# Reading an expert's first weights in 4 KB runs instead of 8 KB runs

## The chip, the core and the metric

The kernel runs on one core of a Trainium2 chip. The metric is the time of one execution on the device, in microseconds, as the median of several runs. A core has a matrix engine (TensorE, PE in the profile; its weight loads are listed as PEld), a vector engine (VectorE, DVE), a scalar engine (ScalarE, ACT), a general engine (GpSimd, POOL) and SyncE (SP), each with its own instruction queue. They share an on-chip memory of 128 partitions (SBUF) and an accumulation memory that TensorE writes to (PSUM). Data comes from the chip's large memory, and goes back to it, by DMAs that run on 16 DMA engines.

## What is computed

Attention over 8 batches with 8 heads, 576 positions and a head dimension of 64, in FP32. Half of the heads use a plain causal window of 32, the other half a causal window of 128 with a dilation of 4. Its output, put together as 4608 rows of 512, goes into a soft mixture of 8 experts with 4 slots each:

```python
logits = x @ phi
d = softmax of logits over the rows
slot_input = d.T @ x                       # 32 slots x 512
for e in range(8):
    h = np.maximum(slot_input[e] @ w1[e], 0.0)   # 512 -> 1024
    slot_out[e] = h @ w2[e]                      # 1024 -> 512
c = softmax of logits over the slots
out = c @ slot_out                         # 4608 x 512
```

The expert weights are w1 with 8 x 512 x 1024 values and w2 with 8 x 1024 x 512, all in FP32 in memory.

## The kernel before

Every load is a DMA issued from POOL's queue. It reads FP32 and writes FP16, so 4 KB in SBUF is 8 KB in the large memory. The output is converted the other way. There are about a hundred DMAs, and they use eight completion semaphores in turn: a DMA that takes a semaphore waits until the DMA that had it before, eight issues earlier, has landed. So no more than about eight loads are under way, and POOL waits at most of its issues.

The order of the program is written out by hand (a schedule with `slot0`, `slot1` and `slot2` for every batch, L565 to L649). While batch b is computed, the loads for batch b + 2 are issued: q and k (`load_qk`, L133) in `slot0`, v (`load_v`, L147 and L150) in `slot1`. Between them `weights` (L531) issues one w1 load (`load_w1`, L212) in each of these two slots. There are 16 w1 loads, two for each expert: two in the prologue, twelve in the slots of the first six batches and two in the seventh. All of w2 follows in the last two batches: L219 loads w2 of an expert as a whole or some of its partitions, L227 loads w2 of the experts 6 and 7 in column halves. Expert 0's w2 is loaded as 96 partitions and four times 8 partitions (`load_w2_eight`, L523), each of these followed by a DMA of 8 x 8 values into a tile `turn` that nothing computes with.

What POOL does besides issuing is small copies: `spread_v` (L205 and L209) follows a w1 load in its queue and places part of v.

The three stages of the mixture are these. `back_u` (L452) adds up `slot_input` before its division, in PSUM, as five column blocks: for every block of 128 features, the features' values x are the matmul's weights and the exponentials stream. `x` of a batch is kept as 256 plain and 256 dilated features. `siTm` (L672) holds the divided result. The w1 product (L686) uses, for each of four `dc`, 128 features on the partitions against `w1t[e][:, dc, :]`. The w2 product (L722, tile `so`) needs w2 of all experts, in the order `ORDER`, 6 and 7 last, and what it gives is combined with the exponentials and sent out (L738 to L802).

So that a partition reads 8 KB in one run, `load_w1` gives partition p the rows 2p and 2p + 1 of a block of 256 rows. The chunk `dc` then holds every second feature, and `back_u` picks every second feature as its weights to match.

Of the kernel before, what the change touches and what calls it, by code (L numbers as in the profile page):

```python
# [32 lines left out]
NT = 5  # L33
# [16 lines left out]
def kernel(  # L50
# [10 lines left out]
    nc = tc.nc  # L61
# [25 lines left out]
    w1t = [w1_pool.tile([128, 4, FDIM], FP16, name=f"w1_{e}", tag=f"w1_{e}") for e in range(E_EXP)]  # L87
# [13 lines left out]
    for i in range(NV):  # L101
        slab = fix.tile([128, V_SLAB], FP16, name=f"v{i}", tag=f"v{i}")
        n = NT * 4 * VW
# [105 lines left out]
        nc.gpsimd.tensor_copy(out=vL[b % NV][0:32, :, :, 0:D], in_=vD[b % NV][96:128, :, :, 0:D])  # L209

    def load_w1(e, i):
        nc.gpsimd.dma_start(  # L212
            out=w1t[e][:, 2 * i : 2 * i + 2, :].rearrange("p l f -> p (l f)"),
            in_=moe_w1[e, 256 * i : 256 * i + 256].rearrange("(p l) f -> p (l f)", l=2),
        )

    def load_w2(e, half=None, rows=slice(0, 128)):
        if half is None:
# [77 lines left out]
    xp_t, xd_t, o_t = {}, {}, {}  # L296
# [140 lines left out]
    def back_u(b):  # L437
        up = ring.tile([128, 5, N_SLOTS], FP32, name=f"u_{b}", tag="ring")
        er = er_t.pop(b)
        jobs = []  # L440
        for t in range(NT):
            n = 128 if t < 4 else TAIL
            for c in range(2):
                x = xp_t[b][0:n, t, :].rearrange("p (x l) -> p l x", l=2)
                jobs.append((c, x[:, c, :], er[0:n, t, :]))
            jobs.append((4, ones[0:n, :], er[0:n, t, :]))
        for r in range(DIL + 1):
            for c in range(2):
                x = xd_t[b][:, r, :].rearrange("p (x l) -> p l x", l=2)
                jobs.append((2 + c, x[:, c, :], er[:, NT + r, :]))  # L450
        for i, (c, l, rr) in enumerate(jobs):
            nc.tensor.matmul(  # L452
                up[:, c, :], l, rr, start=(i == 0), stop=(i == len(jobs) - 1), skip_group_check=True
            )
        if b == 0:
            nc.vector.tensor_copy(out=UT, in_=up)
        else:
            nc.vector.tensor_tensor(out=UT, in0=UT, in1=up, op=ALU.add)
# [4 lines left out]
    def prologue():  # L463
# [47 lines left out]
        for _ in range(2):  # L511
            load_w1(*next_w1.pop(0))
# [18 lines left out]
    def weights(b, g):  # L531
        if b < B - 2:
            load_w1(*next_w1.pop(0))
        elif b == B - 2:
            if g == 0:
                while next_w1:
                    load_w1(*next_w1.pop(0))
                load_w2(0, rows=slice(0, 96))
                load_w2(1)
                load_w2_eight(0)  # L540
            else:
                slab_weights(4, "vs0", V_SLAB)
                load_w2(4)
                load_w2_eight(1)
        elif g == 0:
            raw_pool.release()
            pool = tc.alloc_tile_pool(name="w2b", bufs=1, side="right")
            late_pools.append(pool)
            for e in (2, 3):
                w2t[e] = pool.tile([128, 8, DMODEL], FP16, name=f"w2_{e}", tag=f"w2_{e}")  # L550
                if e == 2:
                    load_w2(e)
        else:
            load_w2(3)
            load_w2_eight(2)
            slab_weights(5, "vs1", V_SLAB)
            load_w2(5)
            load_w2_eight(3)
            slab_weights(6, "qk0", QK_SLAB)
            slab_weights(7, "v0", V_SLAB)  # L560
            for half in range(2):
                for e in HALVED:
                    load_w2(e, half)

    def slot0(b):  # L565
# [34 lines left out]
        if b2:  # L600
            back_u(b - 2)
# [62 lines left out]
    for g in range(4):  # L664
# [8 lines left out]
        out=diag,  # L673
# [7 lines left out]
    for fc in range(2):  # L681
        for g in range(2):
            for dc in range(4):
                for j in range(4):
                    e = 4 * g + j
# [170 lines left out]
```

The softmax here doesn't subtract the row's maximum and nothing guards it: scores larger than these inputs give would overflow.

## Time and profile before

| what | value |
|---|---|
| time, median of 12 runs | 184.9 us (184.06 to 185.39) |
| time of the profiled execution | 184.23 us |
| its span, from the first to the last instruction | 182.1 us |
| PE busy | 143.5 us, 79% |
| DVE busy | 107.3 us, 59% |
| ACT busy | 90.4 us, 50% |
| POOL busy | 85.3 us, 47% |
| memory read, written | 61.93 MB, 9.44 MB |
| w1 DMAs | 16 of 512 KB (as written), 16.8 us from issue to landing |

The page of a profile has the busy time of each engine, then the span in 40 equal slices (each digit is a slice's busy share in tenths, a 9 being 90% or more; below them stand the share of the DMA engines and the GB/s that they moved, counted in SBUF's bytes for loads and in the output's bytes for stores). It then gives the chain of work that ended last, followed back from the last instruction, and the costliest groups of instructions. In a group, x16 is the number of instructions, and what stands behind "idle before" names what ended the engine's wait.

### The profile page before, as it was taken

The page shows a single profiled execution, that of the slowest core. Times are in us where ns is not written, and L with a number is a line of the kernel's source. Part 1 is how long each engine was busy: PE and PEld are TensorE (multiplying, and loading weights), DVE is VectorE, ACT ScalarE, POOL GpSimd, SP SyncE. Part 2 cuts the span into 40 slices and gives each one's busy share as a digit, 9 for nine tenths or more (in the row PEclk, how much of TensorE's full clock was granted, in tenths as well). Part 3 has the DMA queues.
Part 4 walks back from the last instruction along what each step waited for, and adds up shares of the span by engine and source line. Part 5 has one row for each costly group of instructions (what it writes and reads, how often), then busy time and mean ns, then how long its engine had stood idle before and what let it go on. Part 6 is the DMA issues. An engine that isn't in the chain of part 4 may idle for free.

```text
span 182.1 us, 5580 instructions
## 1 busy us (share of the span) xinstructions
PE 143.5 (79%) x2464; PEld 85.6 (47%) x2464; DVE 107.3 (59%) x232; ACT 90.4 (50%) x162; POOL 85.3 (47%) x126
## 2 busy tenths in 40 slices
PE   0467987999999999999999999999879648874000
PEld 0134554656646746746746746747343324331000
DVE  4689786865875985985985985445041105697000
ACT  2044355847657657657657657655101105795000
POOL 7953654624523534533631346514412425999700
PEclk9999997897899999999999999997557995899655
DMA  4999999999999999999999999999999999999991
GB/s 62 195 194 211 205 209 215 201 211 216 199 212 218 198 213 214 206 208 215 202 211 213 203 215 216 212 212 212 215 213 215 194 196 176 372 407 408 411 407 36
DMA packets 29527, 40.75 MB, mean 224 GB/s; under 512 B 1856, under 2 KB 19264, under 8 KB 29504
## 3 DMA queue, kind: packets, MB, share of 16 engines
q0 software_dynamic: 29504, 40.41, 117.7%
q8 instruction: 19, 0.31, 0.6%
q14 instruction: 4, 0.03, 0.0%
HBM read 61.93 MB, written 9.44 MB: 392 GB/s over the span
## 4 chain that ended last, share of the span: by engine, by line
DMA 76%; POOL 6%; issue 6%; PE 3%; DVE 2%; POOLq 1%; ACT 0%
DMA w<-in_moe_w_dram 26%; DMA vs<-in_v_dram 25%; DMA raw<-in_q_dram 20%; DMA out_dram<-of 4%; DVE of L795 2%; PE f L756 2%; POOL raw L138 1%; PE so L722 1%; POOL raw L133 1%; POOL out_dram L802 1%; POOL v L205 1%; POOL v L209 1%; POOL masks L489 1%; POOLq L851 1%; POOL w L212 0%
## 5 line engine op out<-in xcount | busy, mean ns | idle before, releaser
L293 ACT ACTIVATE p<-sa 128x960 f16<-128x960 f32 (+2 forms) x24 | 21.4, 890 | 31.0 <-PE sb L282 30.2
L339 PEld LDWEIGHTS <-p 128*128 128x128 f16 (+2 forms) x544 | 19.7, 99 | 12.8 <-issue 8.6
L245 DVE STREAM_TRANSPOSE qk<-raw 128x320 uint32<-128x320 uint32 (+1 forms) x32 | 21.6, 679 | 0.3
L212 POOL DMA_DIRECT2D w<-in_moe_w_dram x16 | 8.8, 553 | 26.6 <-DMA vs<-in_v_dram 13.8
L293 ACT ACTIVATE p<-sb 128x960 f16<-128x960 f32 (+2 forms) x24 | 21.2, 885 | 0.0
L271 PE MATMUL sa<-masks,ident 128*128 128x480 f16 (+2 forms) x48 | 14.5, 388 | 7.3 <-POOL masks L489 6.2
L236 DVE STREAM_TRANSPOSE qk<-raw 128x576 uint32<-128x576 uint32 x16 | 19.8, 1249 | 0.0
L408 PE MATMUL lg<-xTd,phi 128*128 128x288 f16 x32 | 18.3, 659 | 0.0
L282 PEld LDWEIGHTS <-qk 32*128 32x128 f16 x832 | 12.3, 98 | 11.2 <-issue 8.9
L271 PEld LDWEIGHTS <-ident 128*128 128x128 f16 x96 | 9.1, 106 | 17.8 <-issue 6.5
L339 PE MATMUL o_p<-v,p 128*128 128x65 f16 (+1 forms) x288 | 16.7, 203 | 0.8 <-ACT v L172 0.7
L282 PE MATMUL sa<-qk 32*128 32x160 f16 (+4 forms) x416 | 16.2, 215 | 0.8 <-DVE qk L236 0.8
L282 PE MATMUL sb<-qk 32*128 32x160 f16 (+4 forms) x416 | 16.3, 215 | 0.0
L361 DVE TENSOR_TENSOR xp<-o_p,rc_p 128x448 f16<-128x448 f32 (+1 forms) x24 | 14.5, 602 | 0.8
L361 DVE TENSOR_TENSOR xd<-o_d,rc_d 128x448 f16<-128x448 f32 (+1 forms) x24 | 14.4, 602 | 0.8
L271 PE MATMUL sb<-masks,ident 128*128 128x480 f16 (+2 forms) x48 | 14.4, 386 | 0.2 <-ACT p L293 0.2
L219 POOL DMA_DIRECT2D w<-in_moe_w_dram x10 | 6.7, 671 | 16.5 <-DMA w<-in_moe_w_dram 9.5
L163 PE MATMUL va<-vs,orders 32*128 32x256 f16 (+1 forms) x96 | 12.1, 289 | 1.0 <-ACT p L293 1.0
L412 ACT ACTIVATE ET<-lg 128x288 f16<-128x288 f32 x16 | 6.6, 410 | 12.3 <-PE lg L408 12.1
L209 POOL COPY v<-v 32x1024 f16<-32x1024 f16 x8 | 8.3, 1033 | 7.5 <-DVE v L202 5.7
L382 ACT COPY xTp<-rp 128x576 f16<-128x576 f16 x16 | 10.4, 648 | 1.8 <-PE rp L377 1.8
L227 POOL DMA_DIRECT2D w<-in_moe_w_dram x8 | 5.9, 748 | 10.9 <-DMA w<-in_moe_w_dram 10.9
(103 smaller groups left out, 276.2 us busy)
## 6 DMA issues: line engine op xcount, KB each, us to landing
w<-in_moe_w_dram POOLq DMA_DIRECT2D x16, 512.0 KB, 16.8
w<-in_moe_w_dram POOLq DMA_DIRECT2D x5, 1024.0 KB, 19.3
out_dram<-of POOLq DMA_DIRECT2D x10, 512.0 KB, 6.2
vs<-in_v_dram POOLq DMA_DIRECT2D x8, 512.0 KB, 17.1
raw<-in_q_dram POOLq DMA_DIRECT2D x7, 576.0 KB, 18.2
raw<-in_k_dram POOLq DMA_DIRECT2D x7, 576.0 KB, 18.9
out_dram<-ot POOLq DMA_DIRECT2D x15, 256.0 KB, 4.9
w<-in_moe_w_dram POOLq DMA_DIRECT2D x8, 256.0 KB, 9.6
```

Of the source, the lines that this page charges most:

```text
L163: nc.tensor.matmul(o.rearrange("p (h d) -> p h d", h=4), l, st[:, 0:4, D * r : D * r + D], start=(r == 0), stop=(r == DIL - 1), skip_group ...
L209: nc.gpsimd.tensor_copy(out=vL[b % NV][0:32, :, :, 0:D], in_=vD[b % NV][96:128, :, :, 0:D])
L212: nc.gpsimd.dma_start(out=w1t[e][:, 2 * i : 2 * i + 2, :].rearrange("p l f -> p (l f)"), in_=moe_w1[e, 256 * i : 256 * i + 256].rearrange( ...
L236: nc.vector.transpose(out=dst, in_=src)
L245: nc.vector.transpose(out=o, in_=i)
L271: nc.tensor.matmul(sps[h // 2][:, h % 2, 0:n], ident, bias[g], start=True, stop=False, skip_group_check=True,)
L282: nc.tensor.matmul(sps[h // 2][:, h % 2, c0 : c0 + w], kt_[32 * h : 32 * h + 32, k0 : k0 + 128, tt], qt_[32 * h : 32 * h + 32, q0 : q0 + w ...
L293: nc.scalar.activation(out=pt, in_=sps[ab][:, :, 0:n], func=AF.Exp, scale=SCALE)
L339: nc.tensor.matmul(o[p0 : p0 + np_, n, :], l, rr, start=(k == 0), stop=(k == len(jobs) - 1), skip_group_check=True,)
L361: nc.vector.tensor_tensor(out=x.rearrange("p t (h d) -> p (t h) d", h=4)[0:nq, u0:u1, :], in0=o[0:nq, 0:n, 0:D], in1=rc[0:nq, 0:n, None].b ...
L382: nc.scalar.copy(out=xTp_t[b][:, c, :], in_=rg)
L408: nc.tensor.matmul(lp, phi4[:, kc].rearrange("p c s -> p (c s)"), rhs, start=(kc == 0), stop=(kc == 3))
```

## The change

A partition reads one row of 4 KB from each of two blocks of 128 rows, instead of two rows in one run of 8 KB. A w1 DMA covers the same 256 rows as before, the same 1 MB of memory and the same 512 KB of SBUF, as two runs for each partition. A chunk `dc` now holds 128 features that follow each other, and `back_u` takes packed columns as its weights. The DMAs of expert 0's w2 in pieces of 8 partitions are in both kernels.

```diff
     def load_w1(e, i):
-        nc.gpsimd.dma_start(
-            out=w1t[e][:, 2 * i : 2 * i + 2, :].rearrange("p l f -> p (l f)"),
-            in_=moe_w1[e, 256 * i : 256 * i + 256].rearrange("(p l) f -> p (l f)", l=2),
-        )
+        src = moe_w1[e].rearrange("(c p) f -> p c f", p=128)
+        nc.gpsimd.dma_start(out=w1t[e][:, 2 * i : 2 * i + 2, :], in_=src[:, 2 * i : 2 * i + 2, :])
...
             for c in range(2):
-                x = xp_t[b][0:n, t, :].rearrange("p (x l) -> p l x", l=2)
-                jobs.append((c, x[:, c, :], er[0:n, t, :]))
+                jobs.append((c, xp_t[b][0:n, t, 128 * c : 128 * c + 128], er[0:n, t, :]))
...
             for c in range(2):
-                x = xd_t[b][:, r, :].rearrange("p (x l) -> p l x", l=2)
-                jobs.append((2 + c, x[:, c, :], er[:, NT + r, :]))
+                jobs.append((2 + c, xd_t[b][:, r, 128 * c : 128 * c + 128], er[:, NT + r, :]))
```

## The prediction

> **What bounds the kernel now.** I read the slices and the queue lines of the page first, then the chain that ended last, then the stretches of the span in which only one kind of load is moving, and last the group of the issues that the change touches.
>
> ```profile
> PE   0467987999999999999999999999879648874000
> DMA  4999999999999999999999999999999999999991
> GB/s 62 195 194 211 205 209 215 201 211 216 199 212 218 198 213 214 206 208 215 202 211 213 203 215 216 212 212 212 215 213 215 194 196 176 372 407 408 411 407 36
> DMA packets 29527, 40.75 MB, mean 224 GB/s; under 512 B 1856, under 2 KB 19264, under 8 KB 29504
> ...
> DMA 76%; POOL 6%; issue 6%; PE 3%; DVE 2%; POOLq 1%; ACT 0%
> ```
>
> The DMA row stands at 9 from the second slice to the last but one: the 16 engines never run dry. The GB/s row is not flat inside that. It swings between about 195 and 215 while inputs are loaded (bytes as written, in FP16; the reads are FP32, twice that), and is near 408 once the output is written. The chain agrees: 76% of it is DMA. PE is as full as DMA until slice 29, so it has to be shown which of the two sets the end:
>
> ```profile
> 118.98 20.52 DMA w<-in_moe_w_dram
> ...
> 140.05 0.73 POOL w L227
> 140.78 9.63 DMA w<-in_moe_w_dram
> ...
> 150.45 0.43 PE so L722 x4
> ```
>
> These are pieces of the chain in order of time (start, length, what). The last piece of w2 lands at 150.41; only then can PE do its last four `so` matmuls and the output begin. The timeline has the attention's last matmuls done at 132.5 us, the w1 products (L686) from 134.6 to 140.5, and the `so` matmuls of L722 stopping four times for a DMA, 3.9 us in all. So PE arrives early and waits: the end of the load stream sets the end, and a load stream that is longer by x makes the kernel longer by x.
>
> The speed of each kind of load, from stretches that hold that kind alone (start:end, length, busy time of the engines, granted clock, DMA share, GB/s):
>
> ```profile
> 13.60:17.20 3.60, 2.42 (x20) 1.20 (x20) 3.50 (x5) 1.49 (x4) 1.74 (x3) 1.00 1.11 212
> 40.60:43.40 2.80, 2.52 (x49) 1.66 (x50) 1.69 (x5) 2.08 (x4) 0.71 (x1) 1.00 1.11 211
> 54.20:57.80 3.60, 3.38 (x77) 2.41 (x76) 1.90 (x6) 2.36 (x3) 1.00 (x2) 1.00 1.09 209
> 67.60:70.00 2.40, 2.40 (x60) 1.71 (x59) 1.47 (x5) 1.46 (x3) 0.71 (x1) 1.00 1.12 214
> 118.00:128.00 10.00, 9.46 (x136) 6.14 (x129) 4.49 (x12) 5.34 (x10) 3.09 (x5) 0.87 1.07 213
> 128.00:140.00 12.00, 10.17 (x140) 5.10 (x142) 2.75 (x10) 1.20 (x3) 2.64 (x4) 0.54 1.06 213
> 144.80:151.00 6.20, 2.82 (x75) 2.07 (x73) 0.00 (x0) 0.10 (x1) 2.05 (x3) 0.87 1.45 196
> ```
>
> The first four are q and k (runs of 1152 elements, 2304 B as written), the next two are w2 in whole rows (2048 elements, 4096 B), the last is w2 in halves (256 elements, 512 B). Longer runs go faster, but by little.
>
> **What the Trainium skill says.** "DMA: Bandwidth & Descriptors", section "Why small descriptors are slow", names a fixed overhead of about 3 cycles per packet inside a DMA engine. The trace agrees in kind and nearly in size: below, these stretches give 3.8 ns. "HBM Reference", section "Specifications", puts a core that streams alone at about 425 GB/s; 213 GB/s written in FP16 is 426 GB/s read. There is thus no slack in the memory for shorter runs to use. "TensorE: Matmul & The Clock Gate", section "Weight-path perf modes", says that fast weight loads read packed or strided columns; the strided loads of L452 take 97 ns here against 96 ns for the packed `ones`.
>
> **The change part by part.** The built order of instructions is the same on all five engines, with the same waits. What differs is the shape of 16 DMAs, and the column stride of the matmul weights at L452. The four 8-partition pieces of expert 0's w2 are in both kernels alike, so they cost and bring nothing.
>
> *Packets.* What a packet is follows from counts: v is 8 x 128 x 8 + 8 x 16 x 8 = 9216 runs of 512 B, halved w2 8 x 128 x 4 = 4096, the narrow output 16 DMAs' worth of 256 rows of 1 KB = 4096; with the 1856 under 512 B that makes 19264, the page's figure. So one packet is one run as written, and w1 has 16 x 128 = 2048 of them, of 4 KB. After, it has 4096 of 2 KB.
>
> *Price of a packet.* An engine's time for one packet is 16 x bytes / rate. At 512 B: 16 x 512 / 196 = 41.8 ns; at 4096 B: 16 x 4096 / 213 = 307.7 ns. A straight line through both has 0.0742 ns per byte and a constant of 3.8 ns. It can be tested at 2304 B: 3.8 + 170.9 = 174.7 ns, 211 GB/s; the four stretches of q and k average 211.3. Their reads are runs of 4608 B, close to the new 4096 B, so the line holds where it is needed. Two packets of 2 KB then cost 2 x 155.8 = 311.6 ns, against 307.7 for one of 4 KB: 1.25% slower on w1.
>
> *Sum.* 2048 more packets x 3.8 ns / 16 engines = 0.49 us. The last digit of 196 and 213 lets the constant lie between 3.6 and 4.0 ns, so 0.46 to 0.52 us. All of it lies in the stream whose end sets the end, and none is beside other work. A check with the bytes: w1 is 8.39 MB, 39.4 us at 213 GB/s, and 1.25% of that is again 0.49.
>
> *Issue on POOL.* An issue of L212 takes 557 ns with 128 runs; q and k issues at L133, with 256 runs, take 711. So each L212 grows by about 154 ns, 2.5 us of POOL over the 16. Behind them wait the copies of L205 and L209 and the next q, k and v loads.
>
> ```profile
> L212 POOL DMA_DIRECT2D w<-in_moe_w_dram x16: 527/557/563, 10.8 to 96.3; - x16
> ...
>   DMA vs<-in_v_dram: 13.8, 6
> ...
> DMA to landing us min/median/max: 14.0/16.8/19.1
> ```
>
> I cost this at nothing: the issue of L212 mostly comes after POOL has waited for an earlier DMA to land (1.8 to 2.8 us a time), and it lands 16.8 us after it is issued, with some seven other DMAs queued before it. A delay of 0.15 us shortens that queue and does not empty it. Were there no queue, 2.5 us would be the cost; below zero it cannot be.
>
> *Weights of L452.* The strided loads become packed: 160 loads x 1 ns at most = 0.2 us of PE, which waits for DMA later anyway. Taken as 0; at the other bound, 0.2 us gained.
>
> Against the profiled execution: 184.23 + 0.49 = 184.72 us (span 182.1 + 0.5 = 182.6, and the 2.1 us around it). That execution was 0.7 us below the median of the 12 runs, 184.9; the forecast for the median is 184.9 + 0.5 = 185.4 us. What a measurement of this kernel can tell from no change is about 0.2%, or 0.37 us, so the effect is just above that.
>
> **The rivals.** First, no change. The DMA share column is over 1, so an engine's packets overlap, and the constant could belong to what surrounds short packets (reads in runs of 1 KB) and be gone above some length. Against it: 2304 B lies on the line, with reads of 4608 B. If the constant vanished for 2 KB runs: 184.9 us.
>
> Second, faster. The rates of w1 were never seen alone: its loads always share the stream with v, q or k. The 4 KB packets shown are w2's. If an engine with two outstanding packets of 2 KB keeps its two sides fuller than with 4 KB ones (the share is 1.09 to 1.12 for q and k, 1.07 for w2), then the per-packet constant is not added but saved. Of the line only the 3.8 ns of the old packets can go: 2048 x 3.8 / 16 = 0.5 us, which gives 184.4 us. It decides as soon as a 2 KB packet takes less than half of 307.7, that is under 153.8 ns or over 213 GB/s. For it: one stretch of q and k at 214. Against it: their mean of 211.3.
>
> Third, much slower. The two rows of a partition now lie 128 x 4 KB = 512 KB apart. The Trainium skill ("DMA: Bandwidth & Descriptors", section "Latency and other measured facts") has copies at a row pitch of 512 KiB at 207 GB/s against 214 for a padded one, 3.3% less. An estimate from that page: 3.3% of 39.4 us is 1.3 us, so 186.2 us. Against it: that is a pitch from partition to partition, which here is 4 KB; and w2's two halves of a partition lie 1 MB apart in this trace and still run at 213.
>
> **How the numbers follow.** The packet price, 0.3 to 0.7 us with the scatter of a median: 0.64, of which 0.06 falls inside the 0.2%. No change: 0.17. Faster: 0.11. Row pitch: 0.08. Slower is then 0.58 + 0.08 = 0.66; same 0.06 + 0.17 = 0.23; faster 0.11. The time is that of the likeliest case, 185.4. The range from 184.7 to 186.0 holds the first two and part of the third's neighbours, and leaves out most of the faster case and of the full row pitch, under 2 in 10.
>
> **What would show it.** The page after should have 31575 packets, 19264 of them under 2 KB as before, and the same megabytes. The last w2 piece should land near 150.9 instead of 150.4, with everything after it shifted by the same amount and unchanged in length. L212 should take about 710 ns. The stretches of w2, q and k should keep their rates; only those with w1 in them may lose. I am wrong if w2 lands at 150.4 or before with these packets, if the DMA row shows a slice below 9 before slice 34 (then POOL's issue mattered), or if the loss comes after 151 us.

## The result and the profile after

| | before | after |
|---|---|---|
| median | 184.7 us (183.9 to 185.4, 49 runs) | 183.4 us (182.7 to 184.4, 12 runs) |
| ratio | | 0.993, 95% interval 0.9916 to 0.9945 |
| profiled execution, its span | 184.23, 182.1 us | 183.29, 181.2 us |
| packets of the software queue | 29504 | 31552 |
| mean issue of a w1 DMA | 553 ns | 716 ns |

The change made the kernel faster by 0.7%, 1.3 us. The forecast was slower by 0.5 us. The page of the kernel after, in the lines that the prediction had named (chain shares, DMA share, GB/s, packets):

```profile
DMA  4999999999999999999999999999999999999997
GB/s 62 196 197 208 202 215 209 203 210 213 201 209 212 205 210 211 205 209 215 201 209 212 203 209 214 215 213 213 215 214 210 202 195 171 308 396 410 407 407 181
DMA packets 31575, 40.75 MB, mean 225 GB/s; under 512 B 1856, under 2 KB 19264, under 8 KB 31552
...
DMA 42%; PE 34%; DVE 6%; ACT 6%; POOL 5%; issue 3%; POOLq 1%
```

The packets are the 31575 that were forecast. The DMA row is full to the end, and the load slices move between about 195 and 215 GB/s as before. The chain now runs through PE for a third of the span. This is no sign that PE sets the end: followed back, the chain leaves the DMAs at the k load that is issued at 84.33 us, which waited 1.8 us for a transpose of DVE, and goes on through the attention from there. The load stream is as full as before. The pieces of the chain near the end of the loads:

```profile
125.23 20.57 DMA w<-in_moe_w_dram
146.08 1.16 POOL w L225 x2
147.54 8.99 DMA w<-in_moe_w_dram
```

This last piece of w2 lands at 156.53. Its counterpart of before is not in the chain there; the piece that is, the last that the first half of `so` waits for, landed at 150.41 before and at 151.19 after, by the trace. So the loads end later, not earlier. The whole gain lies behind the last output DMA. The view of the program's last line, for the kernel before and then for the kernel after (engine, operation, number; min, median and max in ns; first and last start in us):

```profile
L851 POOLq DRAIN  x3: 51/86/9477, 171.9 to 181.9; - x3
L851 SPq DRAIN  x3: 7/7/7, 179.4 to 181.7; - x3
```

```profile
L847 POOLq DRAIN  x3: 51/86/7714, 172.7 to 180.9; - x3
L847 SPq DRAIN  x3: 7/7/7, 180.2 to 180.7; - x3
```

SP waits for all DMAs and starts its first DRAIN once they have landed: at 179.4 before, at 180.2 after, 0.8 us later. POOL's first DRAIN starts right after its last issues and ends at 171.93 + 9.48 = 181.40 before, but at 172.71 + 7.71 = 180.42 after. All engines then meet, and the program ends 0.7 us later in both. Below, "gap" is the time from SP's arrival at that meeting to the end of POOL's DRAIN, from the trace: 1.95 us before, 0.19 after. That is 1.76 us gained; less the 0.49 that the packets were to cost, it leaves 1.27 of the 1.3 measured.

Where else POOL behaves differently is in the middle of the output. Its timeline before and after (start, length, and in brackets idle time and its releaser):

```profile
166.46 0.72 POOL L778 DMA_DIRECT2D out_dram<-ot  x1
167.39 0.72 POOL L802 DMA_DIRECT2D out_dram<-of  x1 [0.22 <-DVE ot L772]
168.11 0.72 POOL L778 DMA_DIRECT2D out_dram<-ot  x1
169.34 0.72 POOL L802 DMA_DIRECT2D out_dram<-of  x1 [0.52 <-DMA out_dram<-of]
```

```profile
167.11 0.72 POOL L774 DMA_DIRECT2D out_dram<-ot  x1
169.41 0.72 POOL L798 DMA_DIRECT2D out_dram<-of  x1 [1.58 <-issue]
170.12 0.72 POOL L774 DMA_DIRECT2D out_dram<-ot  x1
```

Before, every gap has a reason. After, POOL stands still for 1.58 us with "issue" as the releaser. Part of that is an ordinary wait: the DMA eight issues earlier landed at 167.62 by the trace, and an issue in the output follows such a landing by 0.56 us elsewhere (169.34 in the first list, after a landing at 168.78). About 1.2 us has no cause that the profile shows. An output DMA takes some 5 to 6 us from issue to landing, so eight queued ones cover the pause, and the GB/s row stays at 407 there (third slice from the end). A pause of that kind is also in the kernel before, but at 100 us:

```profile
96.32 0.53 POOL L212 DMA_DIRECT2D w<-in_moe_w_dram  x1 [1.66 <-DMA w<-in_moe_w_dram]
100.61 0.67 POOL L219 DMA_DIRECT2D w<-in_moe_w_dram  x1 [3.77 <-issue]
```

The semaphore that this issue waits for was there at 99.19 by the trace, and issues of this kind follow such a semaphore by 0.28 us elsewhere, so about 1.1 us of the 3.77 has no cause shown.

### The profile page after: what moved, and what is told of

Same layout as the page of the kernel before. It is cut to its first block, busy times and chain, and to the rows that moved or that the text cites. A ratio compares the mean times of both kernels' runs of the same rounds, so it can differ in the third digit from the quotient of the medians.

```text
span 181.2 us, 5580 instructions
## 1 busy us (share of the span) xinstructions
PE 145.1 (80%) x2464; PEld 86.6 (48%) x2464; DVE 107.5 (59%) x232; ACT 90.5 (50%) x162; POOL 88.2 (49%) x126
## 2 busy tenths in 40 slices
DMA packets 31575, 40.75 MB, mean 225 GB/s; under 512 B 1856, under 2 KB 19264, under 8 KB 31552
## 3 DMA queue, kind: packets, MB, share of 16 engines
q0 software_dynamic: 31552, 40.41, 119.8%
## 4 chain that ended last, share of the span: by engine, by line
DMA 42%; PE 34%; DVE 6%; ACT 6%; POOL 5%; issue 3%; POOLq 1%
DMA w<-in_moe_w_dram 28%; DMA raw<-in_k_dram 10%; PE o_p L337 5%; PE lg L406 5%; PE sa L280 4%; ACT p L291 4%; PE sa L269 4%; DMA out_dram<-ot 4%; PE sb L269 4%; DVE qk L243 2%; PE rd L387 2%; PE vb L163 2%; PE va L163 2%; PE u L448 2%; POOL out_dram L798 1%
## 5 line engine op out<-in xcount | busy, mean ns | idle before, releaser
L269 PE MATMUL sa<-masks,ident 128*128 128x480 f16 (+2 forms) x48 | 15.1, 402 | 7.3 <-POOL masks L485 6.2
L213 POOL DMA_DIRECT2D w<-in_moe_w_dram x16 | 11.4, 716 | 17.1 <-DMA raw<-in_q_dram 6.2
L269 PE MATMUL sb<-masks,ident 128*128 128x480 f16 (+2 forms) x48 | 15.2, 403 | 0.2 <-ACT p L291 0.2
L217 POOL DMA_DIRECT2D w<-in_moe_w_dram x10 | 6.7, 667 | 16.2 <-DMA w<-in_moe_w_dram 9.5
L225 POOL DMA_DIRECT2D w<-in_moe_w_dram x8 | 6.0, 749 | 11.6 <-DMA w<-in_moe_w_dram 7.5
```

Source lines behind the costliest of these rows:

```text
L213: nc.gpsimd.dma_start(out=w1t[e][:, 2 * i : 2 * i + 2, :], in_=src[:, 2 * i : 2 * i + 2, :])
L269: nc.tensor.matmul(sps[h // 2][:, h % 2, 0:n], ident, bias[g], start=True, stop=False, skip_group_check=True,)
```

## The experiments

The first theory was only that the gain is the end of POOL's drain and belongs to the program; the rival, that the 4 KB rows or the packed weights save time by themselves.

**Both kernels again.** No edit.

> The kernel before, unchanged, profiled a second time. In the first profile SP was ready to end at 179.5 us and POOL's first drain ended only at 181.4, 1.9 us later; in the changed kernel the two are 180.2 and 180.4. Theory 'drain' (the gain is the wait for POOL's last drain, and it belongs to the program): again 1.7 to 2.1 us between them, time near 184.7. Theory 'chance' (the drain's length differs from execution to execution): a different gap, anywhere from 0.1 to 2 us.

> The changed kernel, unchanged, profiled a second time. Theory 'drain': POOL's drain again ends within 0.3 us of SP being ready, and POOL again pauses some 1.6 us in the middle of the output, where it costs nothing. Theory 'chance': the gap is different. Either way the last load should land 0.6 to 0.9 us later than in the kernel before.

Times 185.2 and 183.4 us. The last lines of the two, before and after:

```profile
L851 POOLq DRAIN  x3: 51/86/9489, 172.8 to 182.8; - x3
L851 SPq DRAIN  x3: 7/7/7, 180.3 to 182.6; - x3
```

```profile
L847 POOLq DRAIN  x3: 51/86/7763, 172.8 to 181.0; - x3
L847 SPq DRAIN  x3: 7/7/7, 180.3 to 180.8; - x3
```

SP arrives at the same time in both, and only POOL's drain differs: it ends at 182.30 (172.81 + 9.49) and at 180.53 (172.77 + 7.76). The gaps are 1.95 and 0.19 once more, to the hundredth. The theory "chance" falls. The expectation on the last load was not borne out: before, it landed at 156.6 this time against 155.8 in the first profile, after at 156.7, so two executions of one kernel differ by as much as the change was to bring.

**Half of the change.** One of the two w1 DMAs of each expert, and the weights that go with it:

```diff
     def load_w1(e, i):
+        if i == 0:
+            src = moe_w1[e].rearrange("(c p) f -> p c f", p=128)
+            nc.gpsimd.dma_start(out=w1t[e][:, 0:2, :], in_=src[:, 0:2, :])
+            return
         nc.gpsimd.dma_start(
...
-                x = xp_t[b][0:n, t, :].rearrange("p (x l) -> p l x", l=2)
-                jobs.append((c, x[:, c, :], er[0:n, t, :]))
+                jobs.append((c, xp_t[b][0:n, t, 128 * c : 128 * c + 128], er[0:n, t, :]))
```

> Only the first of the two w1 DMAs of each expert is read in 4 KB runs, with packed weights for the plain features alone: 1024 more packets, 64 descriptors more on each engine. Price of a packet: loads end 0.25 us later than before. Theory 'drain', if the drain depends on where POOL stands in writing descriptors: the gap at the end is either 1.9 us or 0.2 us and nothing between, so the time is 184.9 or 183.2. Theory 'rows' (a 4 KB run or packed weights save time by themselves): half of the gain, 184.0 us, with the gap at the end between the two.

Measured: ratio 0.9916 (0.9886 to 0.9945). Half of the change gives all of the gain. The timeline of this kernel is shown with its second run, below.

**w2 instead of w1.**

```diff
+        if half is None and e > 0:
+            nc.gpsimd.dma_start(
+                out=w2t[e].rearrange("p (q l) n -> p q (l n)", q=4),
+                in_=moe_w2[e].rearrange("(q p l) n -> p q (l n)", q=4, l=2),
+            )
+            return
         if half is None:
```

> w1 and its weights as before; instead w2 of the experts 1 to 5 is read in 4 KB runs (rows in another order than the w2 product takes them, so this part of the result is another one). 1280 more packets, 80 descriptors more on each engine. Price of a packet: loads end 0.30 us later than before. Theory 'drain' with descriptors as the cause: w1 is not needed for the gain, so a gap of 0.2 us at the end and a time near 183.2. Theory 'rows' (w1 itself is faster): no gain, 185.0 us with the gap of 1.9 us.

Measured: ratio 0.988 (0.9842 to 0.9918), 182.8 us, with w1 and its weights untouched. A gain of this size thus needs neither other rows of w1 nor packed weights. Its last line, the pause in its output, and two stretches in which nearly all packets are now w2's of 2 KB (last column GB/s):

```profile
L857 POOLq DRAIN  x3: 51/86/6283, 174.4 to 181.1; - x3
L857 SPq DRAIN  x3: 7/7/7, 180.6 to 180.9; - x3
```

```profile
172.54 0.71 POOL L808 DMA_DIRECT2D out_dram<-of  x1 [0.60 <-DMA out_dram<-of]
174.39 0.71 POOL L784 DMA_DIRECT2D out_dram<-ot  x1 [1.14 <-issue]
```

```profile
118.00:128.00 10.00, 9.72 (x172) 6.28 (x170) 5.00 (x13) 6.47 (x12) 4.05 (x6) 1.00 1.12 211
128.00:138.00 10.00, 7.94 (x107) 4.81 (x106) 2.65 (x10) 2.13 (x6) 2.64 (x4) 0.50 1.12 212
```

Packets of 2 KB run at 211 to 212 GB/s, where those of 4 KB run at 213. The prediction's line had 2 x 155.8 ns for the pair, which is 210.3: the price of a packet is about right. The pause comes just before the very last issue, and the gap is gone (-0.01 us).

Now a theory with a number could be made. Where a pause falls late, few DMAs are issued after it, and POOL's drain is short. From the traces, the time from the last output's landing to the end of the drain was 2.34 us with 49 DMAs issued since the last pause (before; the one that was held up included), 0.58 with 6 (after), 0.50 with 4 (half of the change) and 0.38 with 1 (w2 instead of w1): a straight line, 0.34 us and 41 ns for each DMA. The theory "clean-up": POOL has something to tidy up for every DMA it has issued, and does that when its descriptor space is used up, and at its drain.

**Fewer and more DMAs.** Both from the kernel before:

```diff
-                load_w2(0, rows=slice(0, 96))
+                load_w2(0)
...
     def load_w2_eight(j):
-        load_w2(0, rows=slice(96 + j, 128, 4))
-        nc.gpsimd.dma_start(out=turn[0:8, 8 * j : 8 * j + 8], in_=moe_w2[0, 0:8, 0:8])
+        return
```

```diff
     def load_w2_eight(j):
         load_w2(0, rows=slice(96 + j, 128, 4))
-        nc.gpsimd.dma_start(out=turn[0:8, 8 * j : 8 * j + 8], in_=moe_w2[0, 0:8, 0:8])
+        for m in range(3):
+            c0 = 8 * (3 * j + m)
+            nc.gpsimd.dma_start(out=turn[0:8, c0 : c0 + 8], in_=moe_w2[0, 0:8, 0:8])
```

(`turn` has 96 columns in the second.)

> The kernel before with expert 0's w2 as one DMA: the four 8-partition DMAs and the four 8 x 8 DMAs are gone, 92 DMAs instead of 100, nearly the same descriptors. Theory 'clean-up' (POOL tidies up after every DMA it issued, about 42 ns each, when its descriptor space runs out and at its last drain; before, some 49 DMAs are left for the end): 41 left, the gap between SP ready and POOL's drain 1.6 us instead of 1.95, time 184.3 if the loads keep their pace. Rival 'fixed' (a drain costs 2 us or nothing): gap 1.95, time unchanged.

> The kernel before with eight more 8 x 8 DMAs beside the four that are there: 108 DMAs, 16 descriptors more on each engine. Theory 'clean-up': 57 left for the end, gap 2.3 us, time 185.0 or a little more. Rival 'fixed': gap 1.95. If the 16 descriptors were enough to make POOL tidy up earlier, the gap would fall to 0.2, which the theory excludes.

Gaps of 1.62 and 2.27 us, as expected, from these lines:

```profile
L850 POOLq DRAIN  x3: 51/86/9187, 171.8 to 181.4; - x3
L850 SPq DRAIN  x3: 7/7/7, 179.3 to 181.3; - x3
```

```profile
L853 POOLq DRAIN  x3: 51/153/9820, 172.4 to 183.1; - x3
L853 SPq DRAIN  x3: 7/7/7, 179.9 to 182.8; - x3
```

Times: 0.9971 (0.9958 to 0.9984) and 1.0048 (1.0029 to 1.0066). Of the 0.9 us that eight more DMAs cost, the gap holds 0.32. Another 0.36 lies behind POOL's drain: by the trace this program ends 1.09 us after it instead of 0.73, and one of the two short DRAINs of POOL that follow takes 153 ns instead of 86. Why is open, and so is the cause of the remaining 0.2.

**Two w1 DMAs alone.**

```diff
     def load_w1(e, i):
+        if e == 0:
+            src = moe_w1[e].rearrange("(c p) f -> p c f", p=128)
+            nc.gpsimd.dma_start(out=w1t[e][:, 2 * i : 2 * i + 2, :], in_=src[:, 2 * i : 2 * i + 2, :])
+            return
         nc.gpsimd.dma_start(
```

> Only expert 0's two w1 DMAs are read in 4 KB runs (its rows are in another order than the weights then, so its part of the result is another one): 256 more packets, 16 descriptors more on each engine. Theory 'clean-up': too few to make POOL tidy up during the output; 51 DMAs are left for the end, gap 2.0 us, loads 0.06 us longer, time 184.8, if anything slower than before. Rival 'rows': an eighth of the gain, 184.5.

Measured: 1.0009 (0.9994 to 1.0023), gap 2.03 us:

```profile
L855 POOLq DRAIN  x3: 51/86/9512, 171.9 to 181.8; - x3
L855 SPq DRAIN  x3: 7/7/7, 179.3 to 181.6; - x3
```

Two of 16 give none of the gain, eight give all of it: a threshold, not a share.

**Half of the change, again.** The edit is the one shown.

> Half of the w1 DMAs in 4 KB runs, once more, for its profile and a closer time. Theory 'clean-up': 64 more descriptors on each engine make POOL tidy up some 4 DMAs before the end; gap 0.1 us, loads 0.25 us longer, time 184.6 + 0.25 - 1.85 = 183.0. Rival 'rows': 184.0.

Measured: 182.7 us, ratio 0.9901 (0.9883 to 0.9919), gap 0.11, and the pause is in the output:

```profile
L854 POOLq DRAIN  x3: 51/86/7442, 172.7 to 180.6; - x3
L854 SPq DRAIN  x3: 7/7/7, 179.9 to 180.4; - x3
```

```profile
168.66 0.72 POOL L781 DMA_DIRECT2D out_dram<-ot  x1
171.18 0.72 POOL L805 DMA_DIRECT2D out_dram<-of  x1 [1.80 <-issue]
```

**The change without its descriptors.** All of the change stays, but three v loads are made of few long runs (they bring other elements of v than the batches need):

```diff
+        if b in (2, 3, 4):
+            flat = v[b].rearrange("h s d -> (h s d)")[0 : 128 * 2048]
+            nc.gpsimd.dma_start(out=slab[:, 0:2048], in_=flat.rearrange("(p n) -> p n", n=2048))
+        else:
             nc.gpsimd.dma_start(
```

> The changed kernel again, timed beside the next two: 183.3 us, the gap 0.2 us.

> The changed kernel with all its 4 KB runs of w1 and its packed weights, but v of the batches 2 to 4 is read as one 8 KB run for each partition (other elements of v than these batches need, so their result is another one). That takes 168 descriptors from each engine, and 2688 packets. Theory 'clean-up': POOL's descriptor space then lasts to the end of the program, no pause in the output, some 45 DMAs are left for the last drain, gap 1.8 us; the loads are 0.64 us shorter than in the changed kernel by the packet price; time 183.3 - 0.6 + 1.6 = 184.2. Rival 'rows' (the 4 KB runs or the packed weights bring the gain): faster than the changed kernel, 182.7, since packets are saved.

The changed kernel took 183.3 us again (0.9932, 0.9912 to 0.9952), with a gap of 0.19. With its 4 KB rows and packed weights all in place, but fewer descriptors, it took 184.4 (0.9989, 0.9979 to 1.0), though it moves its loads in fewer packets. Its last line gives the gap, 1.78 us:

```profile
L851 POOLq DRAIN  x3: 51/86/9332, 171.9 to 181.7; - x3
L851 SPq DRAIN  x3: 7/7/7, 179.4 to 181.5; - x3
```

**Both improvements.** The half change and expert 0's w2 as one DMA.

> The half change together with expert 0's w2 as one DMA (92 DMAs). Theory 'clean-up': POOL still tidies up some 3 DMAs before the end, so the eight DMAs less bring nothing at the end: gap 0.1 us, time 182.7 as with the half change alone. If 42 ns for each DMA were paid somewhere on the path all along, it would be 0.33 us faster, 182.4.

Measured: 182.7 us, ratio 0.9902 (0.9882 to 0.9921), gap 0.07. What eight DMAs less brought in the kernel before, 0.5 us, does not show here: the gap has only 0.11 left to give. The times of the two kernels can be compared to about 0.5 us, so that alone would not settle it.

All kernels together. Descriptors are the packets of the software queue divided by 16 engines. "Since the pause" counts the DMAs issued from the last pause on, that DMA included. "Line" is 0.34 + 0.041 times that, less the 0.39 us that SP takes from the last landing to its arrival. Four of these kernels made the line (before, after, half of the change, w2 instead of w1); the other five ran after it was drawn, with their counts stated ahead.

| kernel | descriptors | since the pause | line | gap measured |
|---|---|---|---|---|
| e3_fewer_descriptors | 1804 | 45 | 1.80 | 1.78 |
| e2_fewer_dmas | 1828 | 41 | 1.63 | 1.62 |
| before | 1844 | 49 | 1.96 | 1.95 |
| e2_two_loads | 1860 | 51 | 2.04 | 2.03 |
| e2_more_dmas | 1860 | 57 | 2.29 | 2.27 |
| e3_half_one_w2 | 1892 | 3 | 0.07 | 0.07 |
| e2_half | 1908 | 4 | 0.11 | 0.11 |
| e1_w2_runs | 1924 | 1 | -0.01 | -0.01 |
| after | 1972 | 6 | 0.20 | 0.19 |

`e2_two_loads` and `e2_more_dmas` have the same number of descriptors, yet gaps of 2.03 and 2.27 with 51 and 57 DMAs since the pause: what the drain has to do goes by DMAs. Where the pause falls goes by descriptors. The first one has the same place in all of the kernels: it comes with the DMA whose descriptors take the count on each engine (a sixteenth of the runs, and one for the completion) past 1024. That is from 1019 to 1032 before, 1022 to 1087 after, 974 to 1039 in the half change, 1013 to 1030 in `e3_fewer_descriptors`. In the last three it is short, 0.4 to 0.5 us, and follows a copy of POOL that the profile names as the releaser. The v load at this point, before (where the count is still below 1024) and after:

```profile
89.88 0.88 POOL L147 DMA_DIRECT2D vs<-in_v_dram  x1
```

```profile
92.82 0.90 POOL L147 DMA_DIRECT2D vs<-in_v_dram  x1 [0.50 <-POOL v L209]
```

The Trainium skill agrees: "SBUF — State Buffer", section "SBUF size: 192, 224, or 256?", reserves 16 KiB of a partition for the rings that POOL's descriptors are written to, and "DMA: Bandwidth & Descriptors", section "Terms", gives 16 B for a descriptor, so an estimate from these pages, if one engine's entries take up one partition's space, is 1024 entries.

The kernels with 1892 or more descriptors came to a second pause before their end, those with 1860 or fewer did not. What stays open is the exact place of the second one (1866 in the kernel after, 1836 in the half change, 1903 in `e1_w2_runs`; this count ends 4 short of the table's). That POOL then has as many free entries as had landed at the first pause would fit the half change (823 landed, so 1847, inside the DMA that takes the count from 1836 to 1853), but not the first profile of the kernel after (880 landed, so 1904, against 1866 to 1883). That POOL's hidden work is a tidying up of finished DMAs is inferred from the line, too; the profile shows only its idle time and its drain.

## Why the prediction was wrong

- The step that failed is in "Issue on POOL": "I cost this at nothing", with 2.5 us as one bound and "below zero it cannot be" as the other. It counted only the time to write more descriptors, which is indeed hidden. It left out that POOL pauses at certain counts of descriptors, and that its drain at the program's end grows with the DMAs issued since the last pause. More descriptors moved the last pause into the output, where eight queued DMAs cover it, and so took 43 DMAs off the drain, where nothing does. On POOL the change was worth -1.76 us at the end.
- With it fell "everything after it shifted by the same amount and unchanged in length". The part after the last output DMA had been taken as part of the stream. The line of POOL's drain, 9.48 us and ending 2 us after SP was ready, stood in the trace of before and was not read.
- The packet count was exact, the issue of a w1 DMA was given as about 710 ns and took 716. The price of a packet is supported by the rate: 211 to 212 GB/s for 2 KB packets against the 210.3 of the line. In the times it is not settled. The gap fell by 1.76 us and the time by 1.3, which leaves about 0.5 us of cost in the changed kernel; but in the half change the two are 1.84 and 1.83, which leaves nothing where 0.25 was expected, with an interval of 0.3 us either way. In the loads' landing time it cannot be seen, since that differs by 0.8 us between two executions of the kernel before.
- The weights of L452 bring nothing: the kernel that keeps them packed without the descriptors lost the gain.
- The rival "faster" had the sign, with a mechanism that did not happen: 2 KB packets are not above 213 GB/s. The rival of the row pitch did not happen either; the loss it asked for, 1.3 us in the loads, is in none of the three profiles of the changed kernel.

## What to carry to other kernels

Look at what stands between the last landing and the end of the span, engine by engine. Here the last piece that the chain of the kernel before lists is this one (start, length, what):

```profile
171.93 0.93 POOLq L851
```

The chain thus stops at 172.9 us, where POOL's last issue ends, and the 2 us of POOL's drain behind the last landing are not in it. Where POOL issues the DMAs, a change of their run lengths changes how many descriptors are written, and in these kernels so when POOL pauses; a pause that falls shortly before the end but under queued DMAs takes that work off the end. Among the kernels that leave nothing out, half of the change was the best, at 182.7 us, with expert 0's w2 as one DMA or without. It is 0.9901 of before, with its interval touching that of the whole change, so that the half is better than the whole is likely but not settled. Fewer packets to pay for would be the reason; it is argued, not shown.

## What had not been expected of the hardware

POOL's drain at the end of the program ends 0.34 us after the last landing, and about 41 ns later for every DMA that POOL issued from its last pause on. The line holds from 1 to 57 DMAs within 0.02 us. The pauses do not show the same price. They came after 43 to 55 DMAs, which at 41 ns each would be 1.8 to 2.3 us. But the time in them that has no cause shown is 0.95 to 1.3 us, and 0.4 to 0.5 us where POOL had just made a copy. So a part of the work may be hidden, or cheaper there; these runs do not tell. Most of the longer pauses show as "issue" in the profile, the shorter ones behind an ordinary releaser.
